# Routing's small stationary operands padded with zeros to the full array, and the last chunk's low part put ahead of the second half of the slot table's comparison

## The chip, the cores and the metric

The kernel runs on 1 core of one Trainium2 chip. The metric is the device time of one execution in microseconds, as the median of several runs.

## What is computed

Three stages follow each other: banded attention, a dense feed-forward layer with an ELU, and a mixture of eight experts whose routing is greedy over the whole matrix of logits.

```python
# attention: 4 batches x 8 heads, 576 positions, 64 wide, a causal window of 64; x is its output as 2304 x 512
h = x @ w_in                                   # 512 -> 2048
x = where(h > 0, h, exp(min(h, 0)) - 1) @ w_out    # 2048 -> 512
logits = x @ w_gate                            # 2304 tokens, 8 experts
cap = 2304 // 8                                # 288 tokens an expert
for idx in argsort(-logits.flatten()):         # largest logit first
    tok, e = idx // 8, idx % 8
    if assigned[tok] >= 0 or counts[e] >= cap: continue
    assigned[tok] = e; counts[e] += 1
out[assigned == e] = relu(x[assigned == e] @ w1[e]) @ w2[e]     # 512 -> 1024 -> 512
```

## The kernel before

Tokens are held in 18 chunks of 128 (`NCH`). Attention and the first layer's tiles (`layer1`) come first. `layer2` multiplies by `w_out`, chunk by chunk: 48 products of 128x128 by 128x512 into one PSUM bank (L482), then an evacuation into a high and a low half-precision part (`xs`) which SyncE writes to a table in DRAM, `x2d` (L472). For all chunks but the last, ScalarE makes a copy and the high part (L493, L494) and GpSimd the low part (L462, `low_parts`). For the last chunk (`c == NCH - 1`) ScalarE makes the high part (L490) and VectorE the low part (L491), straight from PSUM.

The logits do not wait for `layer2`: they are computed by `gate` from the first layer's output. So routing can run while `layer2` is still at work on its last chunks. `routing` is a generator with high priority; each of its `yield W[i]` lets a fixed number of `layer2`'s products (L482) into TensorE's queue before the next product of routing. TensorE's order is therefore written out by the table `W`, and is kept as written.

Routing makes the greedy assignment in seven phases (`for ph in range(E - 1)`). In a phase the time at which the next expert fills up is searched for with five steps (`for s in range(NS)`), each a digit in base 32:

- VectorE computes the digit's distance `D` (L639) and compares it with all 32 values, for all tokens: `ge` (L645, in two halves of which the second is empty here).
- TensorE counts, expert by expert, how many tokens lie at or above each value: six products with `ge` as the stationary operand, 128 rows by 96 columns (L650). VectorE copies the counts as `co` (L654).
- Three products with the constant `third` as stationary operand, 96 rows by 32 columns (L658), add three rows of `co` into one for each value.
- VectorE compares with the capacity: `full`, 32 partitions by 8, and its sum over experts by the accumulator (L660).
- One product spreads the digit over all partitions: in the first four steps with the constant `wt`, 32 rows by 128 columns (L664), into `lo`; in the fifth with the first 32 rows of `ones` (L667), into `hi`.

Between these stand products of `layer2`: 2 between L650 and L658, 2 between L658 and L664, 5 between L664 and the next L650. The rest of a phase (L671 to L727) uses products whose stationary operand has 128 rows and 128 columns (`ones` in L694, `tri` in L696).

After the last phase the slots of the tokens are turned into a list of indices, `idx`: `oh`, `oA`, then the comparison `oB` in two halves (L772), each followed by nine products (L776), and `idx` (L778). `dummies` puts eight products whose result is not used behind them (L571). Then `gather` reads the rows of the experts' tokens from `x2d` by `idx` (GpSimd's indirect DMAs, L839), which needs `idx` and every chunk of `x2d`; `xe_first` transposes the rows of the first expert on TensorE (L852), and the experts' products follow (L903, L888).

`routing_consts` builds the constants on GpSimd earlier, beside attention.

Of the kernel before, what the change touches and what calls it, by code (L numbers as in the profile page):

```python
# [8 lines left out]
F16 = mybir.dt.float16  # L9
BF = mybir.dt.bfloat16  # L10
# [3 lines left out]
OP = mybir.AluOpType  # L14
# [25 lines left out]
def attention_moe_moe2_kernel(ctx: ExitStack, tc: tile.TileContext, q, k, v, w_in, w_out, w_gate, w1, w2, out):  # L40
    nc = tc.nc
# [3 lines left out]
    E = w_gate.shape[1]  # L45
# [3 lines left out]
    CAP = N // E  # L49
    G = 128  # L50
# [154 lines left out]
    def pe(ins):  # L205
        if pinned:
            tc.keep_in_program_order(ins)
# [161 lines left out]
    last = {}  # L369
# [100 lines left out]
    def layer2(t, chunks=None):  # L470
        def out(c, xs):
            nc.sync.dma_start(x2d[c * 128:(c + 1) * 128, :], xs.rearrange("p a d -> p (a d)"))  # L472

        fg = 1024 // tile_n(t)
        for i in range(tile_n(t) // 128) if chunks is None else chunks:
            c = T0[t] // 128 + i
            px = bank("mm", 3)
            m = 0
            for f in range(NF):
                g = GT[t][f // fg]  # L480
                for a, b in ((0, 0), (0, 1), (1, 0)):
                    pe(nc.tensor.matmul(px, g[:, f % fg, a, 128 * i:128 * i + 128], wo[f // 2][:, b, f % 2, :],  # L482
                                        start=m == 0, stop=m == 3 * NF - 1))
                    m += 1
                    yield 216
            xs = work.tile([128, 2, DM], F16, name="xs")
            x32 = work.tile([128, DM], F32, name="r", bufs=3)

            if c == NCH - 1:
                nc.scalar.activation(xs[:, 0], px, AF.Copy, scale=2.0 ** -11)  # L490
                nc.vector.scalar_tensor_tensor(xs[:, 1], px, 2.0 ** -11, xs[:, 0], op0=OP.mult, op1=OP.subtract)  # L491
            else:
                nc.scalar.activation(x32, px, AF.Copy, scale=2.0 ** -11)  # L493
                nc.scalar.activation(xs[:, 0], x32, AF.Copy)  # L494
                later.append((xs[:, 1], x32, xs[:, 0], lambda c=c, xs=xs: out(c, xs)))
                if not pinned:
                    low_parts()
                continue
            out(c, xs)
# [4 lines left out]
    K = 32  # L504
    PHV = 3
    SPL = 6
    NS = 5
    rt = {}

    def routing_consts(pool):  # L510
        r = rt

        def const(nm, shape, dt=F32):
            r[nm] = pool.tile(list(shape), dt, name=nm, bufs=1)
            return r[nm]

        def iota(nm, shape, pattern, base=0, mult=0, dt=F32):
            const(nm, shape, dt)
            nc.gpsimd.iota(r[nm], pattern=pattern, base=base, channel_multiplier=mult,
                           allow_small_or_imprecise_dtypes=True)  # L520


        iota("k32", [128, K, 3], [[1, K], [0, 3]], base=1)
        nc.gpsimd.tensor_scalar(r["k32"], r["k32"], float(K ** (NS - 1)), 1.0, op0=OP.mult, op1=OP.mult)
        iota("k1", [128, K, 3], [[1, K], [0, 3]], base=1, dt=BF)
        iota("k0", [128, K, 3], [[1, K], [0, 3]], dt=BF)
        const("wt", [K, NS - 1, 128], BF)
        for s in range(NS - 1):
            nc.gpsimd.memset(r["wt"][:, s], float(K ** (NS - 1 - s)))

        const("third", [3 * K, 3, K], F16)
        nc.gpsimd.memset(r["third"], 0.0)
        nc.gpsimd.affine_select(out=r["third"], in_=r["third"], compare_op=OP.not_equal, fill=1.0, base=0,
                                pattern=[[-1, 3], [-3, K]], channel_multiplier=1)

        iota("ebase", [128, E], [[CAP, E]])
        nc.gpsimd.tensor_scalar(r["ebase"], r["ebase"], -0.5 - G / 2, 1.0, op0=OP.add, op1=OP.mult)
        const("reset8", [128, NCH, E], BF)
        nc.gpsimd.memset(r["reset8"], 1.0)
        nc.gpsimd.memset(r["reset8"][:, :, 0:1], 0.0)  # L540
        const("reset", [128, E, NCH], BF)
        nc.gpsimd.memset(r["reset"], 1.0)
        nc.gpsimd.memset(r["reset"][:, :, 0:1], 0.0)
        const("tri", [128, 128], BF)
        nc.gpsimd.memset(r["tri"], 1.0)
        nc.gpsimd.affine_select(out=r["tri"], in_=r["tri"], compare_op=OP.is_gt, fill=0.0, base=0,
                                pattern=[[1, 128]], channel_multiplier=-1)
        const("i24", [128, NG, NCH], F16)
        const("i96", [128, NCH // 2, G], F16)
        iota("id", [128, NCH], [[128, NCH]], base=-N // 2, mult=1, dt=F16)  # L550
        const("one", [1, 128])
        nc.gpsimd.memset(r["one"], 1.0)
        const("ones", [128, 128], BF)
        nc.gpsimd.memset(r["ones"], 1.0)
        const("dead", [128, NCH])
        nc.vector.memset(r["dead"], 0.0)
        const("done", [128, NCH, E], BF)
        nc.gpsimd.memset(r["done"], 0.0)

    def bc(ap, n):  # L560
        return ap[:, :, None].to_broadcast([ap.shape[0], ap.shape[1], n])
# [11 lines left out]
    def routing():  # L573
        r = rt
        pool = r["p"]

        def tl(nm, shape, dt=F32, bufs=1):
            return pool.tile(list(shape), dt, name=nm, bufs=bufs)
# [45 lines left out]
        for ph in range(E - 1):  # L624
# [3 lines left out]
            for s in range(NS):  # L628
                ge = tl("ge", [128, NCH // 3, K, 3], BF, 2)
                if s == 0:  # L630
                    D, kk = M, r["k32"]
                else:

                    Mc = M
                    if s < NS - 1:
                        Mc = tl("Mc", [128, NCH], I32, 2)
                        V.tensor_scalar(Mc, M, -(K ** (NS - 1 - s)), None, op0=OP.bitwise_and)
                    D, kk = tl("D", [128, NCH], BF), r["k1" if s < NS - 1 else "k0"]
                    V.tensor_scalar(D, Mc, lo[:, 0:1], float(K) ** (s + 1 - NS), op0=OP.subtract, op1=OP.mult)  # L639
                pc = bank("sc", 2)  # L640
                for g0, g1 in ((0, SPL), (SPL, NCH // 3)):
                    if g0 == g1:
                        continue
                    d = D.rearrange("p (g i) -> p g i", i=3)[:, g0:g1, None, :].to_broadcast([128, g1 - g0, K, 3])
                    cmp = V.tensor_tensor(ge[:, g0:g1], d, kk[:, None].to_broadcast([128, g1 - g0, K, 3]), op=OP.is_ge)  # L645
                    if later and g0 == 0:
                        low_parts(cmp)
                    yield W[3 if g0 == 0 else 4]
                    for g in range(g0, g1):
                        pe(T.matmul(pc[:3 * K, :3 * E], ge[:, g].rearrange("p k i -> p (k i)"),  # L650
                                    C[:, 3 * g:3 * g + 3].rearrange("p i e -> p (i e)"), start=g == 0,
                                    stop=g == NCH // 3 - 1))
                co = tl("co", [3 * K, 3 * E], F16)
                V.tensor_copy(co, pc[:3 * K, :3 * E])  # L654
                yield W[14]
                pk = bank("sc", 2)
                for i in range(3):
                    pe(T.matmul(pk[:K, :E], r["third"][:, i], co[:, i * E:(i + 1) * E], start=i == 0, stop=i == 2))  # L658
                full = tl("full", [K, E + 1], BF)
                V.tensor_scalar(full[:, :E], pk[:K, :E], float(CAP), 0.0, op0=OP.is_ge, op1=OP.max,  # L660
                                accum_out=full[:, E:])
                yield W[5]
                if s < NS - 1:
                    pe(T.matmul(lo[:, 0:1], r["wt"][:, s], full[:, E:], start=s == 0, stop=True, skip_group_check=True))  # L664
                else:
                    hi = bank("tp", 2)
                    pe(T.matmul(hi[:, :E + 1], r["ones"][:K], full, start=True, stop=True))  # L667


            B = tl("B", [128, NCH], BF)  # L670
# [98 lines left out]
        pi = bank("sc", 2, [128, NG])  # L769
        for half in range(2):  # L770
            hs = slice(half * NCH // 2, (half + 1) * NCH // 2)
            tc.keep_in_program_order(V.tensor_tensor(oB[:, hs], bc(sa[:, hs], G), r["i96"],  # L772
                                                     op=OP.is_equal))
            yield W[12 + half]
            for c in range(half * NCH // 2, (half + 1) * NCH // 2):
                pe(T.matmul(pi[:G], oB[:, c], oA[:, :, c], start=c == 0, stop=c == NCH - 1))  # L776
# [190 lines left out]
    rt["p"] = rpool  # L967
    l4, l5 = layer1(4, [slabB] * 8), layer1(5, [slabB] * 2 + [slabA] * 6)
    weave((chain(take(l4, 4), gate(3), l4, take(l5, 4), gate(4), l5), UT * 4))
    W = [1, 4, 3, 5, 0, 2, 6, 6, 12, 4, 16, 2, 2, 0, 2, 28, 9]  # L970

    def fill():
        for _ in range(3):
# [68 lines left out]
```

## Time and profile before

| | |
|---|---|
| median of 3 runs | 782.66 us (780.07 to 783.17) |
| the profiled execution's own time | 781.48 us |
| its span on the core | 779.6 us |
| PE busy | 736.7 us, 94% |
| DVE busy | 427.0 us, 55% |
| ACT busy | 358.9 us, 46% |
| POOL busy | 176.2 us, 23% |

PE is TensorE's products, PEld its loads of the stationary operand, DVE VectorE, ACT ScalarE, POOL GpSimd, SP SyncE. A product is pipelined: its row gives a start and an end, the ends overlap, and the distance from one start to the next is what it costs the queue. "idle before" with a name behind the arrow says whose work ended the wait; "issue" is a wait for nothing that the profile shows. Routing lies between about 416 and 567 us, the experts between about 574 us and the end.

### The profile page before, as it was taken

The page shows a single profiled execution, that of the slowest core. Times are in us where ns is not written, and L with a number is a line of the kernel's source. Part 1 is how long each engine was busy: PE and PEld are TensorE (multiplying, and loading weights), DVE is VectorE, ACT ScalarE, POOL GpSimd, SP SyncE. Part 2 cuts the span into 40 slices and gives each one's busy share as a digit, 9 for nine tenths or more (in the row PEclk, how much of TensorE's full clock was granted, in tenths as well). Part 3 has the DMA queues.
Part 4 walks back from the last instruction along what each step waited for, and adds up shares of the span by engine and source line. Part 5 has one row for each costly group of instructions (what it writes and reads, how often), then busy time and mean ns, then how long its engine had stood idle before and what let it go on. Part 6 is the DMA issues. An engine that isn't in the chain of part 4 may idle for free.

```text
span 779.6 us, 15588 instructions
## 1 busy us (share of the span) xinstructions
PE 736.7 (94%) x6322; PEld 430.1 (55%) x6322; DVE 427.0 (55%) x1001; ACT 358.9 (46%) x857; POOL 176.2 (23%) x272
## 2 busy tenths in 40 slices
PE   5896998899999999999999999999979999999996
PEld 4665776655655555644545444444456566565662
DVE  3799589934233666355553555555626556456530
ACT  4367797847543554444455221010025455354530
POOL 2000000021000435154451433434132121200001
PEclk9798999999999999989999999999989999999999
DMA  9995256436445434001001211120067888877401
GB/s 280 325 220 136 55 108 194 133 83 145 94 115 122 96 55 108 2 2 54 2 14 42 82 54 42 69 82 29 14 125 238 253 271 252 256 208 234 160 28 42
DMA packets 137528, 94.03 MB, mean 121 GB/s; under 512 B 116464, under 2 KB 116464, under 8 KB 137456
## 3 DMA queue, kind: packets, MB, share of 16 engines
q1 hardware_dynamic: 134576, 83.59, 40.0%
q0 software_dynamic: 2880, 9.44, 3.9%
q8 instruction: 50, 0.82, 0.4%
q14 instruction: 22, 0.18, 0.1%
HBM read 73.68 MB, written 9.44 MB: 107 GB/s over the span
## 4 chain that ended last, share of the span: by engine, by line
PE 65%; issue 14%; DVE 11%; ACT 5%; DMA 3%; POOL 2%; SPq 1%; POOLq 0%; DVEq 0%
PE ps_mm L482 23%; PE ps_mm L404 17%; PE ps_mm L903 6%; PE ps_sc L888 3%; PE ps_tp L888 2%; PE ps_pv L312 2%; PE ps_tp L302 2%; PE ps_mm L392 2%; ACT sm L290 1%; POOL out_dram L873 1%; PE ps_sc L650 1%; DVE b L106 1%; ACT slab L111 1%; DVE r L414 1%; DVE slab L106 1%
## 5 line engine op out<-in xcount | busy, mean ns | idle before, releaser
L482 PE MATMUL ps_mm<-slab,g 128*128 128x512 f16 x864 | 210.7, 380 | 0.0
L404 PE MATMUL ps_mm<-xt,slab 128*128 128x512 f16 (+1 forms) x960 | 178.0, 343 | 6.1 <-DVE r L414 5.2
L404 PEld LDWEIGHTS <-slab 128*128 128x128 f16 x960 | 93.3, 100 | 77.7 <-issue 10.9
L482 PEld LDWEIGHTS <-g 128*128 128x128 f16 x864 | 74.2, 98 | 70.8 <-issue 1.6
L903 PE MATMUL ps_mm<-xet,slab 128*128 128x288 f16 (+2 forms) x840 | 101.6, 277 | 0.0
L817 DVE SCALAR_TENSOR_TENSOR slab<-raw,slab 128x512 f16<-128x512 f32 x112 | 73.6, 688 | 39.0 <-ACT slab L816 36.2
L903 PEld LDWEIGHTS <-slab 128*128 128x128 f16 x840 | 75.2, 98 | 25.2 <-issue 6.0
L888 PEld LDWEIGHTS <-h 128*32 128x32 f16 (+2 forms) x768 | 43.1, 98 | 53.0 <-issue 9.8
L407 ACT ACTIVATE r<-ps_mm 128x512 f32<-128x512 f32 x64 | 38.5, 602 | 66.5 <-PE ps_mm L404 59.1
L816 ACT ACTIVATE slab<-raw 128x512 f16<-128x512 f32 x112 | 65.3, 621 | 0.0
L414 DVE TENSOR_TENSOR r<-ps_mm,r 128x512 f32<-128x512 f32 x64 | 44.0, 688 | 36.3 <-POOL r L413 26.8
L419 DVE TENSOR_TENSOR g<-r,g 128x512 f16<-128x512 f32 x64 | 44.6, 700 | 31.8 <-POOL g L418 25.9
L493 ACT ACTIVATE r<-ps_mm 128x512 f32<-128x512 f32 x17 | 10.2, 599 | 107.1 <-PE ps_mm L482 107.1
L290 ACT ACTIVATE sm<-ps_sc,mx 128x128 f32<-128x128 f32 x144 | 50.7, 379 | 17.6 <-DVE mx L288 17.1
L888 PE MATMUL ps_sc<-slab,h 128*32 128x512 f16 (+2 forms) x384 | 53.4, 381 | 0.0
L888 PE MATMUL ps_tp<-slab,h 128*32 128x512 f16 (+2 forms) x384 | 53.0, 380 | 0.0
L909 DVE SCALAR_TENSOR_TENSOR h<-ps_mm,h 128x288 f16<-128x288 f32 x64 | 29.2, 456 | 39.5 <-ACT h L908 39.2
L908 ACT ACTIVATE h<-ps_mm 128x288 f16<-128x288 f32 x64 | 26.2, 410 | 50.9 <-PE ps_mm L903 50.8
L413 POOL TENSOR_SCALAR r<-r 128x512 f32<-128x512 f32 x48 | 38.5, 802 | 38.5 <-ACT r L408 37.7
L462 POOL TENSOR_TENSOR xs<-r,xs 128x512 f16<-128x512 f32 x17 | 20.0, 1177 | 110.0 <-ACT xs L494 79.3
L418 POOL TENSOR_SCALAR g<-r 128x512 f16<-128x512 f32 x48 | 31.4, 655 | 47.0 <-DVE r L414 28.2
L408 ACT ACTIVATE r<-r 128x512 f32<-128x512 f32 x64 | 40.7, 638 | 1.5
(206 smaller groups left out, 984.2 us busy)
## 6 DMA issues: line engine op xcount, KB each, us to landing
raw<-in_moe_w_dram SPq DMA_DIRECT2D x32, 1024.0 KB, 5.6
slab<-in_moe_w_in_dram SPq DMA_DIRECT2D x16, 512.0 KB, 10.5
st<-in_moe_w_out_dram SPq DMA_DIRECT2D x16, 512.0 KB, 5.2
x2d<-xs SPq DMA_DIRECT2D x18, 256.0 KB, 2.0
vp<-in_v_dram SPq DMA_DIRECT2D x34, 128.0 KB, 3.5
qn<-in_q_dram SPq DMA_DIRECT2D x16, 256.0 KB, 3.9
kn<-in_k_dram SPq DMA_DIRECT2D x16, 256.0 KB, 4.8
vn<-in_v_dram SPq DMA_DIRECT2D x16, 256.0 KB, 3.7
```

Of the source, the lines that this page charges most:

```text
L290: nc.scalar.activation(P[c, blk][:, i], SC[blk][:, i], AF.Exp, bias=mx[:, blk, i:i + 1], accum_out=rs[:, blk, i:i + 1])
L404: nc.tensor.matmul(ph[:, i], wi[d, (f + i) // 8][:, a, (f + i) % 8 * 128:((f + i) % 8 + 1) * 128], XT[t][:, b, d, :n], start=m == 0, stop= ...
L407: nc.scalar.activation(r, ph, AF.Relu, scale=-1.0 / A_H)
L408: last["act"] = nc.scalar.activation(r, r, AF.Exp, scale=-1.0).ins
L413: nc.gpsimd.tensor_scalar(r, r, -1.0, A_H, op0=OP.add, op1=OP.mult)
L414: nc.vector.tensor_tensor(r, ph, r, op=OP.max)
L419: nc.vector.tensor_tensor(lo, r, hi, op=OP.subtract)
L482: pe(nc.tensor.matmul(px, g[:, f % fg, a, 128 * i:128 * i + 128], wo[f // 2][:, b, f % 2, :], start=m == 0, stop=m == 3 * NF - 1))
L816: dv(nc.scalar.activation(t[:, 0, c], st[:, g], AF.Copy, scale=64.0))
L817: dv(nc.vector.scalar_tensor_tensor(t[:, 1, c], st[:, g], 64.0, t[:, 0, c], op0=OP.mult, op1=OP.subtract))
L888: nc.tensor.matmul(po[p0 + k:p0 + k + step], H2[e][:, a, f, s0 + k:s0 + k + step], W2[e][f // 2][:, b, f % 2, :], start=m == 0, stop=m == ...
L903: nc.tensor.matmul(ph[:, r], W1[e][d][:, a, f * 128:(f + 1) * 128], XET[e][:, b, d, r], start=m == 0, stop=m == 3 * ND - 1)
```

## The change

Three tiles are made larger and filled with zeros where they were not there before. `third` gets 128 columns in place of 32 (its columns 32 to 127 are zero), so its product writes 128 partitions of PSUM, 96 of them zero. `full` gets 128 partitions, 96 of them zero since no zero reaches the capacity. `wt` gets 128 rows, and `ones` is used whole, so that L664 and L667 sum over 128 rows of which 96 add nothing.

At routing's end the last chunk's low part (L491) is put on VectorE ahead of the second half of the comparison `oB`; the table's entry `W[12]` becomes 999, which lets the rest of `layer2`, its evacuation included, be written out ahead of that second half.

```diff
             if c == NCH - 1:
                 nc.scalar.activation(xs[:, 0], px, AF.Copy, scale=2.0 ** -11)
-                nc.vector.scalar_tensor_tensor(xs[:, 1], px, 2.0 ** -11, xs[:, 0], op0=OP.mult, op1=OP.subtract)
+                last["x2"] = nc.vector.scalar_tensor_tensor(xs[:, 1], px, 2.0 ** -11, xs[:, 0], op0=OP.mult,
+                                                            op1=OP.subtract).ins
...
-        const("wt", [K, NS - 1, 128], BF)
+        const("wt", [128, NS - 1, 128], BF)
...
-        const("third", [3 * K, 3, K], F16)
+        const("third", [3 * K, 3, 128], F16)
         nc.gpsimd.memset(r["third"], 0.0)
         nc.gpsimd.affine_select(out=r["third"], in_=r["third"], compare_op=OP.not_equal, fill=1.0, base=0,
-                                pattern=[[-1, 3], [-3, K]], channel_multiplier=1)
+                                pattern=[[-1, 3], [-3, 128]], channel_multiplier=1)
...
-                    pe(T.matmul(pk[:K, :E], r["third"][:, i], co[:, i * E:(i + 1) * E], start=i == 0, stop=i == 2))
-                full = tl("full", [K, E + 1], BF)
-                V.tensor_scalar(full[:, :E], pk[:K, :E], float(CAP), 0.0, op0=OP.is_ge, op1=OP.max,
+                    pe(T.matmul(pk[:, :E], r["third"][:, i], co[:, i * E:(i + 1) * E], start=i == 0, stop=i == 2))
+                full = tl("full", [128, E + 1], BF)
+                V.tensor_scalar(full[:, :E], pk[:, :E], float(CAP), 0.0, op0=OP.is_ge, op1=OP.max,
                                 accum_out=full[:, E:])
...
-                    pe(T.matmul(hi[:, :E + 1], r["ones"][:K], full, start=True, stop=True))
+                    pe(T.matmul(hi[:, :E + 1], r["ones"], full, start=True, stop=True))
...
-            tc.keep_in_program_order(V.tensor_tensor(oB[:, hs], bc(sa[:, hs], G), r["i96"],
-                                                     op=OP.is_equal))
+            with tc.issue_after(last["x2"]) if half else ExitStack():
+                V.tensor_tensor(oB[:, hs], bc(sa[:, hs], G), r["i96"], op=OP.is_equal)
...
-    W = [1, 4, 3, 5, 0, 2, 6, 6, 12, 4, 16, 2, 2, 0, 2, 28, 9]
+    W = [1, 4, 3, 5, 0, 2, 6, 6, 12, 4, 16, 2, 999, 0, 2, 28, 9]
```

TensorE's queue holds the same instructions in the same order in both kernels; only the shape behind `third` (and of `full`, `wt`, `ones`) differs. In one step of the search, from the last product with `ge` to the product with `wt`, it reads so before:

```order
L650 MATMUL ps_sc<-C,ge 96x24
L482 LDWEIGHTS g
L482 MATMUL ps_mm<-slab,g 128x512
L482 LDWEIGHTS g
L482 MATMUL ps_mm<-slab,g 128x512
L658 LDWEIGHTS third
L658 MATMUL ps_sc<-co,third 32x8
```

and so with the change (lines are one further down):

```order
L651 MATMUL ps_sc<-C,ge 96x24
L482 LDWEIGHTS g
L482 MATMUL ps_mm<-slab,g 128x512
L482 LDWEIGHTS g
L482 MATMUL ps_mm<-slab,g 128x512
L659 LDWEIGHTS third
L659 MATMUL ps_sc<-co,third 128x8
```

Nothing moved here; the product with `third` now writes 128 partitions in place of 32. On VectorE at the end of routing (`sa`, `oh`, `oA` make the two factors of the slot table, `oB` is its comparison, `xs` the last chunk's low part) the rows before are:

```order
L763 SCALAR_TENSOR_TENSOR sa<-gr,sl 128x18
L765 TENSOR_TENSOR oh<-gr,i_1882 128x324
L767 TENSOR_TENSOR oA<-oh,id 128x324
L772 TENSOR_TENSOR oB<-sa,i_1883 128x1152 x2
L491 SCALAR_TENSOR_TENSOR xs<-ps_mm,xs 128x512
L778 TENSOR_SCALAR idx<-ps_sc 128x18
```

and with the change:

```order
L764 SCALAR_TENSOR_TENSOR sa<-gr,sl 128x18
L766 TENSOR_TENSOR oh<-gr,i_1882 128x324
L774 TENSOR_TENSOR oB<-sa,i_1883 128x1152
L768 TENSOR_TENSOR oA<-oh,id 128x324
L491 SCALAR_TENSOR_TENSOR xs<-ps_mm,xs 128x512
L774 TENSOR_TENSOR oB<-sa,i_1883 128x1152
L779 TENSOR_SCALAR idx<-ps_sc 128x18
```

The low part stands one comparison earlier, the second comparison and `idx` behind it one low part later, and the first comparison now stands ahead of `oA`.

## Rows read from the trace of the kernel before

**Rows 1.** Stretches: length, busy (count) of PE, PEld, DVE, ACT, POOL; PEclk, DMA, GB/s.
```profile
416.00:562.00 146.00, 144.77 (x926) 64.98 (x927) 78.60 (x340) 22.69 (x39) 52.25 (x75) 1.00 0.14 50
...
574.00:577.00 3.00, 2.57 (x25) 2.30 (x24) 0.69 (x1) 0.59 (x1) 2.15 (x3) 0.50 0.71 208
...
582.00:778.00 196.00, 191.37 (x1504) 112.78 (x1500) 101.06 (x176) 94.03 (x193) 29.84 (x29) 1.00 0.64 194
```

**Rows 2.** Timeline, TensorE: start us, length us, engine, line, operation, tiles, shapes.
```profile
417.35 7.94 PE L482 MATMUL ps_mm<-slab,g 128*128 128x512 f16 x36
```

**Rows 3.** Timeline of one step of the search, in the first phase; same columns.
```profile
430.48 1.15 POOL L462 TENSOR_TENSOR xs<-r,xs 128x512 f16<-128x512 f32 x1 [1.45 <-issue]
...
430.75 0.59 PE L482 MATMUL ps_mm<-slab,g 128*128 128x512 f16 x2
430.94 0.18 DVE L654 CAST co<-ps_sc 96x24 f16<-96x24 f32 x1 [0.59 <-PE ps_sc L650]
...
431.27 0.23 PE L658 MATMUL ps_sc<-co,third 96*32 96x8 f16 x3
...
431.43 0.61 PE L482 MATMUL ps_mm<-slab,g 128*128 128x512 f16 x2
...
431.63 0.07 DVE L660 DVE_READ_ACCUMULATOR full<-ps_sc 32x1 bf16 x1
...
431.97 0.17 PE L664 MATMUL ps_pv<-full,wt 32*128 32x1 bf16 x1
...
432.08 1.25 PE L482 MATMUL ps_mm<-slab,g 128*128 128x512 f16 x5
432.18 0.24 DVE L639 TENSOR_SCALAR D<-Mc,ps_pv 128x18 bf16<-128x18 int32 x1 [0.48 <-PE ps_pv L664]
...
433.07 0.22 PEld L650 LDWEIGHTS <-ge 128*96 128x96 bf16 x2 [0.24 <-DVE ge L645]
...
433.17 0.22 PE L650 MATMUL ps_sc<-C,ge 128*96 128x24 bf16 x2
```

**Rows 4.** Timeline, TensorE: three products with full-size `ones` and what follows.
```profile
438.73 0.23 PE L694 MATMUL ps_sc<-mc,ones 128*128 128x48 bf16 x3
438.80 1.46 PE L482 MATMUL ps_mm<-slab,g 128*128 128x512 f16 x6
```

**Rows 5.** By line, whole span: count, then duration in ns min/median/max, first and last start.
```profile
L658 PEld LDWEIGHTS <-third x105: 92/93/96, 425.9 to 554.0; 96*32 96x32 f16 x105
...
L664 PE MATMUL ps_pv<-full,wt x28: 172/172/173, 426.6 to 552.0; 32*128 32x1 bf16 x28
...
L694 PEld LDWEIGHTS <-ones x21: 95/97/98, 438.5 to 556.2; 128*128 128x128 bf16 x21
```

**Rows 6.** Timeline of a step in the sixth phase.
```profile
542.26 1.16 POOL L462 TENSOR_TENSOR xs<-r,xs 128x512 f16<-128x512 f32 x1
...
542.84 0.61 DVE L639 TENSOR_SCALAR D<-Mc,ps_pv 128x18 bf16<-128x18 int32 x1 [0.48 <-PE ps_pv L664]
```

**Rows 7.** Timeline of routing's end.
```profile
563.99 2.62 DVE L772 TENSOR_TENSOR oB<-sa,i 128x1152 f16<-128x1152 f16 x2
564.19 0.60 ACT L490 ACTIVATE xs<-ps_mm 128x512 f16<-128x512 f32 x1 [10.79 <-PE ps_mm L482]
...
566.52 0.68 DVE L491 SCALAR_TENSOR_TENSOR xs<-ps_mm,xs 128x512 f16<-128x512 f32 x1
...
567.18 0.18 DVE L778 TENSOR_SCALAR idx<-ps_sc 128x18 int32<-128x18 f32 x1
...
570.23 1.19 POOL L839 DMA_INDIRECT xe<-x2d,idx  x1 [12.70 <-DMA x2d<-xs]
```

**Rows 8.** The chain of waits that ended last, at routing's end: start us, us, what.
```profile
567.24 2.04 DMA x2d<-xs
```

**Rows 9.** Waits of TensorE from 567 us on: us in total, times, longest.
```profile
PE ps_tp L852 <- DMA xe<-x2d,idx: 3.8, 2, 3.3
```

**Rows 10.** Timeline of GpSimd behind the constants.
```profile
178.12 1.16 POOL L462 TENSOR_TENSOR xs<-r,xs 128x512 f16<-128x512 f32 x1 [17.57 <-ACT xs L494]
```

## Prediction, before the change was run

> **What bounds the kernel now.** The stretches come first [rows 1]. From 416 to 562 us, where routing runs beside the last chunks of layer 2, TensorE is busy for 144.77 of 146.00 us at a granted clock of 1.00 (2.4 GHz), VectorE for 78.60. So the length of this stretch is the length of TensorE's queue, and VectorE has slack on the whole. From 582 to 778 us, the experts, TensorE is busy for 191.37 of 196.00 us. The table of waits from 567 us on has one kind of wait for TensorE, 3.8 us in two, on the gathered rows [rows 9]. Nothing in the experts waits for a fixed moment, so what routing saves should arrive whole at the end of the kernel.
>
> A busy TensorE is not one that works at full pace, so the next view is the timeline. Left alone, products of layer 2 follow each other at 0.216 us: 36 of them take 7.94 us, of which the last one's own length, 0.38 us, is to be taken off before dividing by 35 [rows 2]. With that yardstick one step of the search is read [rows 3]. Two products of layer 2 start at 430.75, so the queue is free again at 430.75 + 0.43 = 431.18. The next one, with `third`, has its data by then (`co` is done at 430.94 + 0.18 = 431.12), and yet starts at 431.27: 0.09 us late. From there the next product of layer 2 starts 0.16 us on, at 431.43. Three products with a stationary operand of full size need only 0.07 for the same [rows 4], so 0.08 is lost. From 431.43 two products again need 0.43, and the one with `wt` starts at 431.97, after 0.54: 0.11 lost. `full` was done at 431.70, so the data are not the reason here either. From `wt` to the next product it is 0.11, where a third of that 0.07 would do: 0.08 lost. The last five take 1.09 against 1.08: 0.01 lost. Together TensorE loses 0.09 + 0.08 + 0.11 + 0.08 + 0.01 = 0.37 us of a step of 2.67, always on the way into or out of a product whose stationary operand has 32 rows or 32 columns, and never around `ones` at full size. All of these four operands become full-size with the change.
>
> **The change part by part.** There are 35 steps (105 loads of `third` at three a step), 28 with `wt`, the other 7 with `ones` [rows 5].
>
> *Into `third` to `wt` or `ones`.* I take that the losses go with the shape: 0.09 + 0.08 + 0.11 = 0.28 us in each of 35 steps, 9.8 us. VectorE doesn't eat this up. `co` is ready 0.06 before the queue is free. `full` ends 0.43 after `third` starts (431.70 against 431.27), and the product that needs it comes 0.07 + 0.43 = 0.50 after it.
>
> *Out of `wt` to the next `ge`.* TensorE would be there 0.03 + 1.08 = 1.11 after `wt`, in place of 1.20. But here VectorE is next in line: the load of `ge`, which follows the end of the comparison, starts at 433.07, 1.10 after `wt` [rows 3]. With the time from that load to its product this is a tie or a wait of some hundredths, so I count 0.07, not 0.09, in 28 steps: 2.0 us. Behind `ones` in the fifth step VectorE and GpSimd have a longer chain before the next product of routing. I count nothing there, at most 7 x 0.09 = 0.6.
>
> *Given back.* In the sixth phase `D` takes 0.61 us where it takes 0.24 elsewhere, and it ends at 543.45, just after a low part on GpSimd that ran from 542.26 to 543.42 [rows 3, 6]. I read this as the two excluding each other. There the step's gain, 0.35, is lost. Elsewhere the low part ends before `D`: in the step of [rows 3] at 431.63 with `D` at 432.18, which comes 0.28 earlier, so 0.27 of margin stays. That margin is what is late next: a low part that begins a quarter of a microsecond later in its step would hold `D` back by a few hundredths.
>
> *Dearer work.* `full` goes from 32 to 128 partitions with the same 8 elements in each; the products' moving operands keep their 8, 1 and 9 columns. I count nothing. The larger constants cost GpSimd some tenths once, and behind them it idles for 17.57 us [rows 10]: nothing.
>
> The Trainium skill, "TensorE: Matmul & The Clock Gate", section "LDWEIGHTS (loading the stationary operand)", speaks against this change: a load takes its number of columns divided by 1.2, in ns. An estimate from that page is 107 ns in place of 27 for each of 105 loads, 8.4 us more if it lay bare, and the sum would end near 778.5. The trace does not agree that the time goes by columns: 92 to 96 ns at 32 columns, 95 to 98 at 128.
>
> *The end of routing.* Before, VectorE makes both halves of the comparison from 563.99, then the low part from 566.52, and `idx` at 567.18 [rows 7]. ScalarE's high part was ready at 564.19 + 0.60 = 564.79, so the low part can follow the first half, (566.52 - 563.99) / 2 = 1.27 us earlier. The transfer to `x2d` is issued at 567.24 and lands 2.04 later, 569.28 [rows 8]; now 565.97 and 568.01. `idx` comes 0.68 later, done at 567.18 + 0.18 + 0.68 = 568.04. The first gather started 0.95 after the landing, at 570.23, and its row names that transfer as what it waited for [rows 7]. It now waits for the later of two things that come nearly together, 568.0 to 568.1: a gain of 1.15 us. The ends are 0.5 (should the way from `idx` be longer than that from the landing) and 1.3. The first comparison ahead of `oA` only swaps two neighbours whose results are needed together.
>
> *The clock.* From 574 to 577 us TensorE is busy for 2.57 of 3.00 us at 0.50, 1.2 GHz [rows 1], when it transposes the gathered rows. The wait ahead of it gets shorter by the gain and by the later `dummies`. Whether that changes the level I can't tell from one execution; about half of 2.57, 1.3 us, is the price either way, and I count nothing.
>
> **Sum.** 9.8 + 2.0 - 0.35 = 11.4 in the search, 1.15 at its end: 12.6 us. The profiled execution has 781.48 us (span 779.6, the rest around it), which is 1.2 under the median of 782.66 and within the three runs. From the median the sum gives **770.0 us**, from the profiled one 768.9. The search's term lies between 35 x 0.27 + 28 x 0.05 - 0.7 = 10.1 (two collisions, a longer wait for `ge`) and 35 x 0.29 + 28 x 0.09 + 0.6 = 13.3.
>
> **The rivals.**
>
> *A: the 96 rows of `third` still cost a switch.* It is widened to 128 columns but still has 96 rows, a shape that the trace doesn't show. Then only the losses around `wt` and `ones` go: 0.10 of the 0.11 in 35 steps and 0.07 in 28, 5.5 us, less 0.2 given back, plus 1.15: 776.2 us. Against it: `ge` has 128 rows and 96 columns, and layer 2's products run into it at 1.09 for five, so 96 of one dimension does no harm there. The Trainium skill, "TensorEngine Tiling (Array Packing)", section "Available Configurations", knows only 128, 64 and 32 rows or columns for a mode of the array, and by "Key Properties" changing the mode drains it. By that rule the 96 rows always ran in a mode of 128 and the columns alone made the switch, which lowers this rival's chance.
>
> *B: the stall belongs to the wait and not to the shape.* `third` and `wt` are products that wait for VectorE; if TensorE pauses at such a wait anyway, padding does nothing and only the end's 1.15 stays: 781.5 us. Against it: `full` was done 0.27 before `wt` started, and the way out of both products is slow too, where nothing is waited for.
>
> *C: slower.* The pauses stay as in B, and the wider loads are not hidden: TensorE can't load ahead while it pauses, so each of the 105 loads of `third` lies bare with its 98 ns in place of the 0.025 at which full-size products follow each other. That is 0.073 x 105 = 7.7 us more, less 1.15: 789.2 us. It decides as soon as a load shows 0.011 us more with the pauses in place; with the pauses gone it would have to show 12.6 / 105 = 0.12. Against it: the three full-size products of [rows 4] follow each other within 0.07.
>
> **How the numbers follow.** The forecast has a chance of 0.80, A 0.09, B 0.06, C 0.04; 0.01 is left for no change from another cause. A measurement of this kernel can tell about 0.5% from no change, 3.9 us, so 778.7 and 786.6 are the bounds. The forecast and A are faster, 0.89; B and the rest are the same, 0.07; C is slower, 0.04. The range goes from 767.0 (both terms at their upper ends, 14.6, and 1.1 of the clock's) to 776.5 (A).
>
> **What would show it.** In the new trace `third` should start 0.43 to 0.45 after the first of the two products before it (0.52 before), the next product of layer 2 0.07 to 0.08 after `third` (0.16), `wt` 0.43 to 0.44 after that (0.54), and the next `ge` 1.11 to 1.15 after `wt` (1.20); a step is 2.30 to 2.35 us long. The low part should start some 1.3 us ahead of where it stood against the first comparison, and the gather should follow the later of `idx` and the landing by about 0.95. Rival A shows as `third` still at 0.52 with `wt` at 0.44; B as all four unchanged; C as `third` to the next product at 0.3. The forecast is wrong if the steps shorten as said and the gather does not come 12 us earlier, or if the time from gather to end grows.

## The result, and the profile after

The changed kernel takes 771.56 us (median of 4 runs, 769.45 to 773.29) against 782.60 us (780.07 to 783.17). The ratio is 0.9859, 95% interval 0.9826 to 0.9892: 11.0 us less. In a second comparison it was 0.9841 (0.9819 to 0.9863).

The profiled execution has 772.79 us, a span of 770.9. Its stretches, with the columns of [rows 1]: routing's search, and the transposes of the gathered rows:

```profile
427.00:554.00 127.00, 125.30 (x887) 60.84 (x885) 75.35 (x324) 19.06 (x32) 51.12 (x74) 1.00 0.16 57
...
565.00:568.00 3.00, 2.57 (x25) 2.31 (x24) 0.69 (x1) 0.71 (x1) 2.34 (x3) 0.50 0.71 212
```

TensorE is as busy in the search as before, which says little: the same instructions pass in less time. The transposes run at 0.50 (1.2 GHz) as they did before [rows 1]. The timeline of one step, to be laid beside [rows 3]:

```profile
429.90 0.44 PE L651 MATMUL ps_sc<-C,ge 128*96 128x24 bf16 x6
429.99 1.15 POOL L462 TENSOR_TENSOR slab<-raw,slab 128x512 f16<-128x512 f32 x1 [5.80 <-DVE ge L646]
430.19 0.59 PE L482 MATMUL ps_mm<-slab,g 128*128 128x512 f16 x2
...
430.41 0.34 PEld L659 LDWEIGHTS <-third 96*128 96x128 f16 x3
430.62 0.22 PE L659 MATMUL ps_sc<-co,third 96*128 96x8 f16 x3
...
430.70 0.59 PE L482 MATMUL ps_mm<-slab,g 128*128 128x512 f16 x2
...
431.13 0.17 PE L665 MATMUL ps_pv<-full,wt 128*128 128x1 bf16 x1
431.16 1.24 PE L482 MATMUL ps_mm<-slab,g 128*128 128x512 f16 x5
431.37 0.24 DVE L640 TENSOR_SCALAR D<-Mc,ps_pv 128x18 bf16<-128x18 int32 x1 [0.31 <-PE ps_pv L665]
...
432.26 0.21 PEld L651 LDWEIGHTS <-ge 128*96 128x96 bf16 x3 [0.35 <-DVE ge L646]
432.26 0.26 PE L651 MATMUL ps_sc<-C,ge 128*96 128x24 bf16 x2
```

`third` starts 0.43 us after the first of the two products before it (0.52 before), the next product 0.08 after `third` (0.16), `wt` 0.43 after that (0.54), the next product 0.03 after `wt` (0.11). All four losses are gone. The next `ge` comes 1.13 after `wt` (1.20), and its load and its product start together at 432.26: here the queue now waits for VectorE. Before, the load started 0.10 ahead of the product [rows 3].

The rows of the loads show where the time around `third` went. Before, its load had this row:

```profile
431.27 0.14 PEld L658 LDWEIGHTS <-third 96*32 96x32 f16 x3 [0.42 <-issue]
```

It started together with its product at 431.27, although no load had run for 0.42 us and the constant was long there. With the change it starts at 430.41, 0.21 ahead of its product, beside the products before it, and it is so in all 35 steps (0.00 before, 0.21 now). Why such a load doesn't run ahead at a change of shape, no row shows.

The end of routing, to be laid beside [rows 7] and [rows 8]:

```profile
555.60 0.32 DVE L766 TENSOR_TENSOR oh<-gr,i 128x324 f16<-128x324 f16 x1
555.84 1.35 DVE L774 TENSOR_TENSOR oB<-sa,i 128x1152 f16<-128x1152 f16 x1
...
557.10 0.32 DVE L768 TENSOR_TENSOR oA<-oh,id 128x324 f16<-128x324 f16 x1
557.34 0.68 DVE L491 SCALAR_TENSOR_TENSOR xs<-ps_mm,xs 128x512 f16<-128x512 f32 x1
...
557.94 1.35 DVE L774 TENSOR_TENSOR oB<-sa,i 128x1152 f16<-128x1152 f16 x1
...
559.88 0.18 DVE L779 TENSOR_SCALAR idx<-ps_sc 128x18 int32<-128x18 f32 x1 [0.59 <-PE ps_sc L777]
561.04 1.19 POOL L840 DMA_INDIRECT xe<-x2d,idx  x1 [11.30 <-DMA x2d<-xs]
```

and the chain of waits there:

```profile
558.05 2.03 DMA x2d<-xs
```

The transfer lands at 560.08 and `idx` is done at 560.06. Both ways to the gather are now equally long, and the gather, whose row names the transfer, starts 0.96 after the landing, as it did before (0.95).

The next table cuts each kernel's profiled execution at three points of its timeline: the first product with `ge`, the last product with `tri` (the one that makes the slots, L750 before), the first gather. All times in us.

| kernel | up to the first `ge` | search | last `tri` to gather | gather to end | span |
|---|---|---|---|---|---|
| before | 425.13 | 136.41 | 8.69 | 209.39 | 779.6 |
| changed | 427.50 | 126.25 | 7.28 | 209.90 | 770.9 |
| changed, second execution | 427.12 | 126.27 | 7.28 | 209.75 | 770.4 |
| padding alone | 427.17 | 126.29 | 8.69 | 210.68 | 772.8 |
| end alone | 427.42 | 136.43 | 7.29 | 209.79 | 780.9 |
| `third` alone, and the end | 424.84 | 130.00 | 7.28 | 209.72 | 771.8 |
| `full`, `wt`, `ones` alone, and the end | 425.15 | 132.89 | 7.29 | 210.03 | 775.4 |
| `third` with 64 columns | 426.97 | 133.81 | 7.28 | 210.16 | 778.2 |
| `third` with 96 columns | 427.78 | 127.84 | 7.27 | 210.62 | 773.5 |
| `ge` with 128 columns too | 426.92 | 122.34 | 7.28 | 210.03 | 766.6 |
| index patterns early too | 424.48 | 124.64 | 7.28 | 210.73 | 767.1 |
| all three additions | 425.90 | 120.09 | 7.28 | 211.22 | 764.5 |
| the same, more `dummies` | 423.99 | 120.09 | 7.28 | 209.81 | 761.2 |

The search and the way to the gather repeat to 0.04 us among kernels that have them alike. The first and the last column vary by some us, though next to nothing is edited there: the kernel with the end alone, without any padding, has 427.42 up to the first `ge`, and the one with the wide `third` 424.84. That is why single executions are read by the two columns in the middle, and times only from several rounds.

### The profile page after: what moved, and what is told of

Same layout as the page of the kernel before. It is cut to its first block, busy times and chain, and to the rows that moved or that the text cites. A ratio compares the mean times of both kernels' runs of the same rounds, so it can differ in the third digit from the quotient of the medians.

```text
span 770.9 us, 15588 instructions
## 1 busy us (share of the span) xinstructions
PE 732.0 (95%) x6322; PEld 434.8 (56%) x6322; DVE 427.6 (55%) x1001; ACT 358.9 (47%) x857; POOL 176.3 (23%) x272
## 4 chain that ended last, share of the span: by engine, by line
PE 66%; issue 14%; DVE 9%; ACT 5%; DMA 3%; POOL 2%; SPq 1%; POOLq 0%; DVEq 0%
PE ps_mm L482 23%; PE ps_mm L404 17%; PE ps_mm L904 6%; PE ps_mm L392 3%; PE ps_sc L889 3%; PE ps_pv L312 2%; PE ps_tp L889 2%; PE ps_tp L302 2%; ACT sm L290 1%; POOL out_dram L874 1%; PE ps_sc L651 1%; ACT slab L111 1%; DVE r L414 1%; DVE b L106 1%; PE ps_sc L275 1%
## 5 line engine op out<-in xcount | busy, mean ns | idle before, releaser
L482 PE MATMUL ps_mm<-slab,g 128*128 128x512 f16 x864 | 202.4, 379 | 0.0
```

## The experiments

**The parts of the change, one at a time.** Padding alone: the end of routing goes back to the old text.

```diff
-            with tc.issue_after(last["x2"]) if half else ExitStack():
-                V.tensor_tensor(oB[:, hs], bc(sa[:, hs], G), r["i96"], op=OP.is_equal)
+            tc.keep_in_program_order(V.tensor_tensor(oB[:, hs], bc(sa[:, hs], G), r["i96"],
+                                                     op=OP.is_equal))
...
-    W = [1, 4, 3, 5, 0, 2, 6, 6, 12, 4, 16, 2, 999, 0, 2, 28, 9]
+    W = [1, 4, 3, 5, 0, 2, 6, 6, 12, 4, 16, 2, 2, 0, 2, 28, 9]
```

Expected:

> The padding alone; the end of routing as in the kernel before. Theory 1 (the loss goes with the shape of the stationary operand): the search from the first product with ge to the last product with tri takes 126.3 us as with the whole change (136.4 before), third to wt 0.51 (0.70 before), and from that last product with tri to the first gather 8.7 us as before. Time about 10 us under the kernel before. Theory 2 (part of the gain came from the other order on VectorE): the search stays above 127 us.

Measured: search 126.29, way to the gather 8.69, ratio to the kernel before 0.9846 (0.9795 to 0.9897). From `third` to `wt` it takes 0.51 in the median, as forecast. The padding alone makes the search's gain; theory 2 falls.

The other half alone keeps the new order at routing's end and takes back every padded shape (`third`, `wt`, `full`, the slices of `pk` and `ones`).

> The new order at the end of routing alone, no padding. Theory 1: the search takes 136.4 us as before with third to wt at 0.70, and the last product with tri to the first gather takes 7.3 us in place of 8.7, so 1.4 us less in all, which the times can hardly tell from no change. Rival: the longer pause of TensorE ahead of the gather leaves it at the lower clock for longer, and from the gather to the end of the kernel takes over 0.5 us more than before (209.4), which gives half of the gain back or all of it.

Measured: search 136.43, way to the gather 7.29, ratio 0.9981 (0.9958 to 1.0003). The trace shows 1.40 us less on the way to the gather. The times can't tell it from no change. From the gather to the end it took 209.79, 0.40 more than before, which is less than the spread of that column (209.39 to 211.22), so the traces neither show the rival nor rule it out.

The padding was then split. First `third` alone is wide:

```diff
-        const("wt", [128, NS - 1, 128], BF)
+        const("wt", [K, NS - 1, 128], BF)
...
-                full = tl("full", [128, E + 1], BF)
-                V.tensor_scalar(full[:, :E], pk[:, :E], float(CAP), 0.0, op0=OP.is_ge, op1=OP.max,
+                full = tl("full", [K, E + 1], BF)
+                V.tensor_scalar(full[:, :E], pk[:K, :E], float(CAP), 0.0, op0=OP.is_ge, op1=OP.max,
...
-                    pe(T.matmul(hi[:, :E + 1], r["ones"], full, start=True, stop=True))
+                    pe(T.matmul(hi[:, :E + 1], r["ones"][:K], full, start=True, stop=True))
```

> third has 128 columns, full and wt and ones stay at 32 partitions; the end of routing as changed. Theory 1 (shape, and 96 rows count as full): ge to third 0.68 to 0.72 as with the whole change, third to the next product of layer 2 0.08, that product to wt 0.54 as before (the switch into 32 rows stays), wt to the next 0.11, so third to wt 0.61. Rival (96 rows still cost a switch): ge to third 0.775 and third to the next product 0.16, all as before. Rival (the wait for VectorE costs it): both as before too.

TensorE's timeline of one step:

```profile
432.30 0.40 PE L651 MATMUL ps_sc<-C,ge 128*96 128x24 bf16 x6
432.56 0.59 PE L482 MATMUL ps_mm<-slab,g 128*128 128x512 f16 x2
432.99 0.22 PE L659 MATMUL ps_sc<-co,third 96*128 96x8 f16 x3
433.06 0.59 PE L482 MATMUL ps_mm<-slab,g 128*128 128x512 f16 x2
433.59 0.17 PE L665 MATMUL ps_pv<-full,wt 32*128 32x1 bf16 x1
433.69 1.25 PE L482 MATMUL ps_mm<-slab,g 128*128 128x512 f16 x5
```

Around `third` the losses are gone (0.43 and 0.07 to 0.08), though it still needs `co` from VectorE and still has 96 rows; around `wt`, still with 32 rows, they stay (0.53 and 0.10). In the median `ge` to `third` is 0.684 and `third` to `wt` 0.603. Both rivals fall.

Then the other way round: `third` keeps 32 columns, and `full` is one tile whose lower 96 partitions are set to zero once.

```diff
-        const("third", [3 * K, 3, 128], F16)
+        const("full", [128, E + 1], BF)
+        nc.gpsimd.memset(r["full"], 0.0)
+        const("third", [3 * K, 3, K], F16)
...
-                full = tl("full", [128, E + 1], BF)
-                V.tensor_scalar(full[:, :E], pk[:, :E], float(CAP), 0.0, op0=OP.is_ge, op1=OP.max,
-                                accum_out=full[:, E:])
+                full = r["full"]
+                V.tensor_scalar(full[:K, :E], pk[:K, :E], float(CAP), 0.0, op0=OP.is_ge, op1=OP.max,
+                                accum_out=full[:K, E:])
```

> full, wt and ones have 128 partitions (the 96 lower ones are set to zero once), third stays at 32 columns; the end of routing as changed. Theory 1: ge to third 0.775 and third to the next product 0.16 as before, that product to wt 0.43 to 0.44, so third to wt 0.60, and wt to the next product 0.03. The search is about 136.4 less 35 x 0.10 less 28 x 0.07, some 131 us; with the kernel that pads third alone it shares the gain about evenly. Rival (the wait for VectorE costs it): 0.54 from that product to wt as before.

```profile
430.29 0.44 PE L653 MATMUL ps_sc<-C,ge 128*96 128x24 bf16 x6
430.58 0.59 PE L482 MATMUL ps_mm<-slab,g 128*128 128x512 f16 x2
431.10 0.23 PE L661 MATMUL ps_sc<-co,third 96*32 96x8 f16 x3
431.26 0.60 PE L482 MATMUL ps_mm<-slab,g 128*128 128x512 f16 x2
431.70 0.17 PE L667 MATMUL ps_pv<-full,wt 128*128 128x1 bf16 x1
431.73 1.24 PE L482 MATMUL ps_mm<-slab,g 128*128 128x512 f16 x5
```

The mirror image: 0.52 and 0.16 around `third`, 0.44 and 0.03 around `wt`. But the search took 132.89, not 131. Of the 1.9 us that are missing the rows show about half: the six products with `ge` need 0.29 to the next product of layer 2 (430.29 to 430.58), where they needed 0.26 in the kernel with `third` alone. That is the load of `ge` that no longer runs ahead (below), 0.037 us in 28 steps. Most of the rest lies behind `wt` and `ones`: from `wt` to `ge` 34.74 - 33.42 = 1.3 us were gained where 28 x 0.07 = 2.0 were expected, and from `ones` to the next phase it took 0.3 longer than before. The gains of the two halves, 6.41 and 3.52, add up to 9.93 of the 10.16 us of both.

**How many columns.** `third` with 64 and with 96 columns, in the form with one `full` tile:

```diff
-        const("third", [3 * K, 3, 128], F16)
+        const("third", [3 * K, 3, 64], F16)
...
-                    pe(T.matmul(pk[:, :E], r["third"][:, i], co[:, i * E:(i + 1) * E], start=i == 0, stop=i == 2))
+                    pe(T.matmul(pk[:64, :E], r["third"][:, i], co[:, i * E:(i + 1) * E], start=i == 0, stop=i == 2))
```

> As the whole change, but third has 64 columns. Theory 1a (a step in the number of columns, above 64 counts as full): a switch as before, third to the next product of layer 2 0.16 and not 0.08, and from that product to wt 0.44; the search takes some 35 x 0.17 = 6 us longer than with the whole change, about 132 us. Theory 1b (the loss grows with the columns that are missing): half of that, third to the next product about 0.12.

> As the whole change, but third has 96 columns, as many as ge has. Theory 1a: no switch, ge to third 0.72 as with the whole change; the loads of third then stand 0.045 apart like those of ge in place of 0.026, so third to the next product 0.13 in place of 0.08; the search is about 128 us. Theory 1b: a quarter of the loss of 32 columns is left over, third to the next product about 0.10 and ge to third over 0.72.

With 64 columns (timeline, then the loads by line):

```profile
432.45 0.59 PE L482 MATMUL ps_mm<-slab,g 128*128 128x512 f16 x2
432.97 0.26 PE L661 MATMUL ps_sc<-co,third 96*64 96x8 f16 x3
433.16 0.60 PE L482 MATMUL ps_mm<-slab,g 128*128 128x512 f16 x2
```
```profile
L661 PEld LDWEIGHTS <-third x105: 106/109/113, 427.7 to 553.3; 96*64 96x64 f16 x105
```

With 96 columns:

```profile
432.90 0.59 PE L482 MATMUL ps_mm<-slab,g 128*128 128x512 f16 x2
433.33 0.26 PE L661 MATMUL ps_sc<-co,third 96*96 96x8 f16 x3
433.45 0.59 PE L482 MATMUL ps_mm<-slab,g 128*128 128x512 f16 x2
```
```profile
L661 PEld LDWEIGHTS <-third x105: 121/123/125, 428.2 to 548.2; 96*96 96x96 f16 x105
```

At 64 columns the way into `third` costs what it costs at 32, 0.52, and with 0.19 the way out is 0.03 longer still; the loads are slower too, 109 ns against 93, and start with their product as at 32. So the expected 0.16 and the expected search of about 132 us were too low: the search took 133.81, 7.6 us more than with the whole change, since a step costs 0.21 and not 0.17. At 96 columns there is no switch (0.43). Of the two theories 1a holds: between 64 and 96 columns there is a step, and 64 columns are no better than 32. But 96 columns are not as good as 128: the three products take 0.12 in place of 0.08, and the search 127.84, within 0.2 of what was expected.

**The next load of that kind.** `ge` has 96 columns in 210 loads. Its tile gets 32 columns of zeros at the end, and each load takes 128 columns, the last 32 of them from the next group; the 32 rows of counts that this adds aren't read.

```diff
+        for b in range(2):
+            const("ge%d" % b, [128, 3 * K * (NCH // 3 - 1) + 128], BF)
+            nc.gpsimd.memset(r["ge%d" % b][:, K * NCH:], 0.0)
...
-                ge = tl("ge", [128, NCH // 3, K, 3], BF, 2)
+                wide = r["ge%d" % (s % 2)]
+                ge = wide[:, :3 * K * NCH // 3].rearrange("p (g k i) -> p g k i", k=K, i=3)
...
-                        pe(T.matmul(pc[:3 * K, :3 * E], ge[:, g].rearrange("p k i -> p (k i)"),
+                        pe(T.matmul(pc[:, :3 * E], wide[:, 3 * K * g:3 * K * g + 128],
```

> The whole change, and the stationary operand of the counting products has 128 columns too (32 columns of the next group of values, or of zeros behind the last, whose counts nobody reads). Theory: the spacing of these products of 0.045 comes from loading 96 columns and falls to 0.026 as with third, ge to third from 0.72 to about 0.60, where the copy co is next in line (0.46 after the last of them); the search takes 35 x 0.10 to 0.12 us less, 122.5 us. Rival: the spacing is one of the product with 24 columns and stays at 0.045, nothing changes.

```profile
431.45 0.31 PE L655 MATMUL ps_sc<-C,ge 128*128 128x24 bf16 x6
431.61 0.59 PE L482 MATMUL ps_mm<-slab,g 128*128 128x512 f16 x2
432.04 0.22 PE L663 MATMUL ps_sc<-co,third 96*128 96x8 f16 x3
```
```profile
L655 PEld LDWEIGHTS <-ge x210: 95/95/99, 426.7 to 541.3; 128*128 128x128 bf16 x105
```

The six products take 0.16 in place of 0.29, `ge` to `third` is 0.594 in the median, the search 122.34: 3.9 us less, as expected; the rival falls. The load of 128 columns takes less time than that of 96 (95 ns against 125).

**The collision with the index patterns.** GpSimd's instructions for the patterns are written at the end of the sixth phase, but the slow step beside them, that of [rows 6] too, is the first of the seventh and last phase: GpSimd is still at work on them there. Now the patterns move to `routing_consts`.

```diff
-            if ph == E - 3:
-                for nm, pt in (("i24", [[1, NG], [0, NCH]]), ("i96", [[0, NCH // 2], [1, G]])):
...
-        const("i24", [128, NG, NCH], F16)
-        const("i96", [128, NCH // 2, G], F16)
+        iota("i24", [128, NG, NCH], [[1, NG], [0, NCH]], dt=F16)
+        iota("i96", [128, NCH // 2, G], [[0, NCH // 2], [1, G]], dt=F16)
+        nc.gpsimd.tensor_scalar(r["i96"], r["i96"], 0.5 - G / 2, 1.0, op0=OP.add, op1=OP.mult)
```

> The whole change, and the two index patterns i24 and i96, which GpSimd makes inside the search's sixth phase, are made with the other constants, where GpSimd is idle. Theory (VectorE and GpSimd exclude each other): no step has D above 0.25 or the comparison above 0.57, the longest wt to ge falls from 2.78 to 1.13 and the search by 1.6 us to 124.6. Rival: D and the comparison are slow there for another reason, and stay at 0.87 and 1.50.

The changed kernel has this there:

```profile
535.67 1.16 POOL L462 TENSOR_TENSOR xs<-r,xs 128x512 f16<-128x512 f32 x1
536.00 0.87 DVE L640 TENSOR_SCALAR D<-Mc,ps_pv 128x18 bf16<-128x18 int32 x1 [0.31 <-PE ps_pv L665]
536.92 1.17 POOL L733 TENSOR_SCALAR i<-i 128x1152 f16<-128x1152 f16 x1
536.99 1.50 DVE L646 TENSOR_TENSOR ge<-D,k 128x576 bf16<-128x576 bf16 x1
```

With the patterns made early, by line (min/median/max in ns):

```profile
L647 DVE TENSOR_TENSOR ge<-D,k x28: 549/557/558, 426.3 to 540.4; 128x576 bf16<-128x576 bf16 x28
L641 DVE TENSOR_SCALAR D<-Mc,ps_pv x21: 244/245/246, 425.9 to 537.7; 128x18 bf16<-128x18 int32 x21
```

Both maxima are back at the median, and the search takes 124.64: 1.6 us less, as expected. Each of the two slow instructions had ended shortly after the GpSimd instruction that it overlapped: `D` 0.04 us after the low part, the comparison 0.4 after L733. All ten profiles here with this collision repeat it: `D` takes 0.58 to 0.99 us, and always ends 0.03 to 0.04 after the low part.

**All together.** The two additions, and a third buffer for `Mc`, on one chip with the changed kernel.

```diff
-                        Mc = tl("Mc", [128, NCH], I32, 2)
+                        Mc = tl("Mc", [128, NCH], I32, 3)
```

> The changed kernel once more, on the same chip as the two that follow. Theory: 10 to 12 us under the kernel before, the search at 126.2 us and from the last product with tri to the gather 7.3; what its runs differ by lies ahead of the search (first product with ge at 424.5 to 427.8 us in the traces so far) and follows the granted clock there.

> The changed kernel with three more edits: 128 columns for the counting products, the index patterns made early, and a third buffer for Mc so that all three are made in a phase's first step. Theory: the first edit gives 3.9 us and the second 1.6, as each did alone; the third takes the longest wt to ge of each phase from 1.20 to 1.13, 7 x 0.08 = 0.5 us. The search is 126.25 - 3.9 - 1.6 - 0.5 = 120.2 us, the time 6 us under the changed kernel. Rival: the steps are now so short that GpSimd's low part (1.15 us, from the end of a comparison on) runs into the next D, some D rise above 0.25 us, and less than 5 us is left.

| kernel, 5 rounds | median us | ratio to before | interval |
|---|---|---|---|
| changed | 771.68 | 0.9841 | 0.9819 to 0.9863 |
| with the three additions | 766.41 | 0.9777 | 0.9758 to 0.9795 |

The changed kernel repeats as expected, 12.0 us under the one before with a search of 126.27. With the three additions the search takes 120.09 us, where 120.2 was forecast, and all values of `D` stay at 0.25. The times show 5.3 us of the 6 expected against the changed kernel, and the search shows all of it. The low part on GpSimd now ends 0.11 us before `D` starts (431.58 and 431.69 in the step below); in the changed kernel's step above it was 0.23 (431.14 and 431.37), so shorter steps would soon run into it:

```profile
430.43 1.15 POOL L462 TENSOR_TENSOR xs<-r,xs 128x512 f16<-128x512 f32 x1 [1.07 <-issue]
...
431.69 0.24 DVE L645 TENSOR_SCALAR D<-Mc,ps_pv 128x18 bf16<-128x18 int32 x1 [0.31 <-PE ps_pv L670]
```

This version beats both kernels: 17.2 us under the one before (783.65 in that comparison) and 5.3 under the changed one.

Last, on top of it, products without use to hold the clock: five ahead of each half of the products with `oB`, and 18 in place of 8 behind them.

```diff
-    DM2 = 8
+    DM2 = 18
...
             yield W[12 + half]
+            dummies(5)
```

> As the one before, with five products without use ahead of each half of the products with oB and 18 in place of 8 behind them. Theory: the granted clock falls to 0.5 at routing's end because TensorE has little to do there; with these it stays at 1.0 up to the transposes of the gathered rows or falls later, and from the gather to the end of the kernel takes 209.4 us or less, against 209.9 to 210.7 with the new order at the end of routing: 0.5 to 1 us. Rival: they hold up the products with oB or the transposes, and the way to the gather (7.3 us) or from it grows.

```profile
552.00:556.00 4.00, 2.23 (x17) 1.09 (x16) 0.00 (x0) 0.00 (x0) 3.08 (x4) 1.00 0.48 137
556.00:560.00 4.00, 3.85 (x61) 3.18 (x60) 0.69 (x1) 1.02 (x1) 3.09 (x4) 1.00 0.82 212
```

Without them, in the version above, the stretch with the transposes reads:

```profile
558.00:563.00 5.00, 4.55 (x43) 4.56 (x44) 0.41 (x1) 1.02 (x1) 3.06 (x4) 0.50 0.83 198
```

With them the granted clock stayed at 1.00 up to and through the transposes, and the way to the gather did not grow. From the gather to the end this execution took 209.81, more than the 209.4 that were expected, and kernels without these products reach it too (209.39 to 211.22). The time is 766.20 (762.95 to 767.64), ratio 0.9769 (0.9741 to 0.9797), the same as without. Inconclusive: the clock was held, a gain from it is not shown.

## Why the prediction was right, point by point

*The shape, not the wait* (chance 0.80): shown by the two halves of the padding, each of which removes its own losses and leaves the other's. Rival A (96 rows still cost a switch) falls with `third` of 96 rows at 0.43. Rival B (the wait costs it) falls with the same row, since `third` needs `co` from VectorE as before. Rival C (bare loads) falls with loads of 128 columns that take 94 to 100 ns and yet let products follow each other at 0.03.

*Into `third` to `wt` or `ones`*, forecast 9.8 us: measured 9.0. From `third` on it came out exactly: 35 times 0.70 became 0.51, 6.7 us. The part from `ge` to `third` was over-sized: forecast 0.09 x 35 = 3.2, measured 27.31 - 24.96 = 2.35 (sums over 35 steps). The step that failed is the sentence that VectorE doesn't eat this up. I had looked at `co` and not at the load of `ge`. When the queue waits for `ge`, the first load starts with its product (432.26 above), and that product needs 0.065 us to the second in place of 0.028. That is 0.037 in 28 of the 35 steps, 1.0 us; in the seven first steps of a phase, where `ge` is ready early, `ge` to `third` is 0.683 as forecast.

*Out of `wt` to `ge`*, forecast 2.0 less 0.35 given back: measured 34.74 - 33.65 = 1.09 (sums over 28 steps). In most steps 1.127 is what was forecast. In the first step of each phase but the last the gain is nothing, 1.204: VectorE makes an `Mc` between `D` and the comparison there. The row that I read was another step. With the third buffer for `Mc` these steps take 1.13, which makes up 0.5 of the 0.56 us that are missing. The collision, which the prediction puts in the sixth phase and which lies in the seventh, ate its step's gain, as forecast, and no more: that one `wt` to `ge` went from 2.50 to 2.78, 0.28 longer, and the step from `ge` to `ge` is 3.98 us long in both kernels.

*The end*, forecast 1.15: measured 1.40. The forecast took 0.12 off the 1.27 of the comparison because `idx` might be late, more than its own rows gave (569.28 - 568.04 = 1.24); `idx` was not late (560.06, the landing 560.08). The other 0.12 is the swap of `oA` and the first comparison, which I had called without effect. These rows are from the kernel before:

```profile
563.39 0.32 DVE L765 TENSOR_TENSOR oh<-gr,i 128x324 f16<-128x324 f16 x1
563.74 0.33 DVE L767 TENSOR_TENSOR oA<-oh,id 128x324 f16<-128x324 f16 x1
```

`oA` started 0.35 after `oh`, which it reads. With the change the comparison, which doesn't read `oh`, starts 0.24 after it, and the low part 0.24 after `oA`. From `oh` to the low part it takes 557.34 - 555.60 = 1.74 us, against 566.52 - 563.39 = 3.13 with both comparisons: 1.39 less, of which one comparison is 1.27. The swap was not run by itself.

*The sum*: forecast 12.6 us and 770.0; measured in the trace 10.16 + 1.40 = 11.6, in the times 11.0 (771.56) and, in the second comparison, 12.0 (783.65 to 771.68). Two terms were over-sized by 0.8 and 0.56 us and the end under-sized by 0.25, so part of the errors cancelled. The prediction also named signs of being wrong. By the letter two of them occurred in the profiled pair: the gather comes 9.2 us earlier (570.23 and 561.04) and not 12, and the time behind it grows by 0.5. The 2.4 us that are missing at the gather against the 11.6 lie ahead of routing, and so the spans differ by only 8.7. Nothing in the change touches TensorE's work in either place. All executions together spread from 424.0 to 427.8 in the first and from 209.4 to 211.2 in the last column, and the changed kernel's four runs go with the granted clock: 772.79 and 773.29 us at a mean of 0.966 and 0.967, 769.45 and 770.33 at 0.982 and 0.977. That the clock is the cause was not tried by itself.

## What to carry to other kernels

A small product in a dense queue can cost several times its own time on the way in and out: `wt` needs 0.03 us to the next product at full size and lost 0.17 more with 32 rows. The yardstick is the distance from one start to the next, against that of undisturbed products. Where its stationary operand has 32 or 64 columns or 32 rows, zeros up to 128 remove that and cost next to nothing here (`full` takes 0.167 us in place of 0.154); even 96 columns are worth padding. Then ask which engine is next in line at each wait, for every kind of step and not for one, since the first step of a loop may hold an instruction that the others don't.

## What the runs showed of the hardware that was not expected

- A load of the stationary operand is not the longer the more columns it has: 93 ns at 32, 109 at 64, 123 at 96 and 96 at 128 columns (medians of 105 loads each, 16-bit). Products with `ge` stood 0.045 us apart at 96 columns and 0.025 at 128. The Trainium skill, "TensorE: Matmul & The Clock Gate", section "Weight-path perf modes — Fast Weight Load (FWL) and DoubleRow", says that a faster load is on when there are 128 weights and the type isn't FP32; these runs agree in that 128 columns load faster than 96.
- The loss at a change of shape is a step: none on the way in at 96 columns, the full 0.09 us at 64 and at 32. The Trainium skill, "TensorEngine Tiling (Array Packing)", section "Key Properties", says that a change of mode drains the engine, and gives no price. That the loss here is such a drain no row shows; its size is 0.19 us for the way in and out with 32 columns (`third` 0.09 later, `third` to `wt` 0.604 against 0.509), 0.21 with 64, and 0.17 with 32 rows (`third` to `wt` 0.603 against 0.509, `wt` to the next product 0.104 against 0.027).
- VectorE's `D` and comparison, 0.24 and 0.56 us long alone, ended in the seventh phase only 0.04 and 0.4 us after the GpSimd instruction that they overlapped, while `co` and `full` ran beside low parts at their usual 0.18 and 0.17 us. The comparison in a phase's first step, which reads 32-bit integers, ran beside GpSimd's update of `dead` (L726) in 0.76 us, against 0.73 alone. So it is not every pair that excludes each other; which do, these runs don't settle.
